# Attention followed by a squared-ReLU feed-forward network: value loads of 128 rows, early softmax work dealt anew, planner costs from occupied times

## The chip, the cores and the metric

The kernel runs on one core of a Trainium2 chip. The metric is the device time of one execution in microseconds (us), lower is better. Before the change three runs took 636.17, 637.12 and 638.25 us, median 637.12 us. The engines are named as in the profile: PE (TensorE matmul), PEld (its weight loads), DVE (VectorE), ACT (ScalarE), POOL (GpSimd) and SP (SyncE, which only issues DMAs here).

## The reference

```python
# attention: q, k, v are (4, 8, 768, 64) float32; block 32, window 16
k_sum = k.reshape(B, H, nb, block, D).max(axis=3)      # 24 block keys: the largest
v_sum = v.reshape(B, H, nb, block, D).mean(axis=3)     # 24 block values: the mean
scores_l = scale * q @ k^T, kept only where |i - j| < 16, else -1e9
scores_s = scale * q @ k_sum^T + log(32)
a = softmax(concat(scores_l, scores_s))                # 94 near keys and 24 block keys matter
x = a @ concat(v, v_sum)                               # -> 3072 tokens x 512
# feed-forward: w_in (512, 2048), w_out (2048, 512), drawn as 64-bit floats
h = x @ w_in ;  out = relu(h)**2 @ w_out               # (3072, 512) float32
```

## The kernel before

**Tiling.** A group g is 64 tokens of one batch with all 8 heads: 12 groups in each of 4 batches, 48 in all. A group needs 118 keys, the 24 block keys and 94 near ones. Eight groups (512 tokens) make a unit u of the feed-forward network, so there are 6 units; each runs over f = 0 to 15, blocks of 128 of the 2048 hidden columns. The start of the program has to push eight groups through attention before the first unit can run whole; its first half (groups 0 to 3) and the blocks f = 0 and 1 are taken in halves "a" and "b" so that something can start earlier.

**Attention of a group.** The names that the planner uses are given in brackets. SP loads the queries (QL, L442) and the values (LV, L449: 96 rows of 2 KB, into partitions 24 to 119 of the group's value tile). PE makes the scores (S, L486; for groups 0 to 7 it adds the mask by a second product). DVE takes the largest of each row (X, L557) and scales it (L561). ACT takes four exponentials with their sums (E, L573). DVE inverts the sums (R, L585 and L586). POOL multiplies (N, L592). PE transposes (T, L604) and ACT copies the result out (A, L611); from group 8 on DVE does the transposition instead (T, L621) with a round trip through memory. POOL copies the 24 block values into the value tile (LS, L455). PE multiplies by the values (V, L648). The result is split in two parts, a high part (XH, L700) and the rest (XL, L703). For groups 0 to 7, which are visited one at a time, both parts are made by DVE. The block values themselves are made once per batch by PE and gathered by four ACT copies (VS, L427); the block keys are made by four DVE reductions over the batch's keys (KL loads, L358; KM, L361).

**Feed-forward.** Weights come as 64-bit floats, 512 KB for each half of a block (WL, L747). They are turned into a high and a low part: ACT (WM, L750), DVE shift (WR, L753), DVE join (WJ, L759), ACT (WH, L764), DVE (WW, L767). PE then makes the hidden product (FI, L813: 12 matmuls), ACT applies ReLU and, in units 0 and 1, the square, ACT and DVE split the result (GH, L830; GL, L833), and PE makes the second product (FO, L843).

**What sets the order.** Each engine's instructions are written in the order that a small planner finds (`Plan.order`): a list scheduler over tasks with a cost, a key (a due time, the smaller the earlier), dependencies and buffers. It keeps a model of the DMA pipe (`DMA_RATE`, `DMA_LATENCY`). Due times come from `T0`, `STEP`, `A0`, `B0`, `HALF_AT`. The engines run their lists strictly in order, so a plan that is off by some time makes an engine wait behind one instruction. The DMA issues also follow each other in a ring: in the trace an issue starts when the eighth issue before it has landed, if that is later.

## Time and profile before

| | |
|---|---|
| time, median of 3 | 637.12 us |
| the profiled execution's own time | 635.87 us |
| its span | 634.2 us |
| PE busy | 613.0 us (97%) |
| DVE busy | 299.6 us (47%) |
| ACT busy | 268.7 us (42%) |
| POOL busy | 78.1 us (12%) |
| granted PE clock | 0.999 of full speed |

The span is from the first to the last instruction; the execution's own time is 1.67 us longer. Engines overlap, so the busy times do not add. A row of a timeline gives the start, the length, the engine, the line, the operation, output and inputs, and in brackets the idle time just before it with what ended it. The chip overlaps the end of one instruction with the start of the next on the same engine, so the time that one occupies is the distance of two starts where the engine is never idle, a little less than its length.

### The profile page before, as it was taken

What the parts mean: (1) busy time and instruction counts of PE and PEld (TensorE: products, weight loads), DVE (VectorE), ACT (ScalarE), POOL (GpSimd) and SP (SyncE); (2) the same over time, 40 slices, a digit from 0 to 9 for tenths busy, and PEclk for the clock granted to TensorE, in tenths of its full rate; (3) what the DMA queues carried; (4) which work ended last, traced back from release to release, by engine and by line L of the source; (5) the groups of instructions that cost most, each with busy time, mean ns of one, the idle gap of its engine ahead of it and who ended that gap; (6) DMA issues with size and microseconds to landing.
All of it is one profiled execution on the core that took longest, in us unless ns stands there. A gap on an engine that the chain in (4) does not pass through costs nothing.

```text
span 634.2 us, 11015 instructions
## 1 busy us (share of the span) xinstructions
PE 613.0 (97%) x4216; PEld 489.4 (77%) x4216; DVE 299.6 (47%) x517; ACT 268.7 (42%) x709; POOL 78.1 (12%) x140
## 2 busy tenths in 40 slices
PE   4779999999999999999999999999999999999997
PEld 3568788778777778777878778778788788888885
DVE  3798979633433433533543644534444432322221
ACT  1888778626544444332432523414343322222221
POOL 4731101101110110101210101201011010000000
PEclk9999999999999999999999999999999999999999
DMA  8998986244324832232415543133323020100001
GB/s 273 257 310 253 357 313 199 91 108 133 92 60 95 280 86 98 67 84 68 104 48 165 171 132 90 48 85 87 103 72 98 16 67 0 68 0 1 1 1 66
DMA packets 55448, 73.65 MB, mean 116 GB/s; under 512 B 6476, under 2 KB 33100, under 8 KB 55396
## 3 DMA queue, kind: packets, MB, share of 16 engines
q1 hardware_dynamic: 55396, 72.95, 39.0%
q8 instruction: 33, 0.54, 0.4%
q14 instruction: 19, 0.16, 0.1%
HBM read 55.56 MB, written 16.78 MB: 114 GB/s over the span
## 4 chain that ended last, share of the span: by engine, by line
PE 92%; DMA 7%; SPq 0%; DVE 0%; ACT 0%; issue 0%; DVEq 0%
PE o L843 42%; PE h L813 42%; PE x L648 3%; PE att L486 3%; DMA qvpa_lent<-qW 3%; DMA raw<-wW 2%; DMA q<-qW 1%; PE vps L415 1%; SPq L358 0%; PE h_0b L813 0%; PE h_1b L813 0%; DVE os L881 0%; ACT os L881 0%; DVE xl L703 0%; SPq L442 0%
## 5 line engine op out<-in xcount | busy, mean ns | idle before, releaser
L813 PE MATMUL h<-xh,w 128*128 128x512 f32 x752 | 236.9, 396 | 0.0
L843 PE MATMUL o<-w,gh 128*128 128x512 f32 x752 | 196.1, 395 | 1.4 <-DVE os L881 0.8
L843 PEld LDWEIGHTS o<-w,gh 128*128 128x128 f32 x752 | 139.7, 188 | 36.6 <-issue 2.7
L813 PEld LDWEIGHTS h<-xh,w 128*128 128x128 f32 x752 | 140.7, 188 | 33.8 <-issue 0.8
L813 PE MATMUL h<-xl,w 128*128 128x512 f32 x376 | 148.8, 396 | 0.0
L822 ACT ACTIVATE r<-h 128x512 f32<-128x512 f32 x94 | 56.2, 598 | 205.9 <-PE h L813 205.6
L833 DVE TENSOR_TENSOR gl<-r,gh 128x512 fp32r<-128x512 f32 x94 | 66.6, 709 | 101.6 <-ACT gh L830 65.5
L828 DVE TENSOR_TENSOR r<-r 128x512 f32<-128x512 f32 x64 | 45.2, 706 | 139.8 <-ACT r L822 139.7
L843 PE MATMUL o<-w,gl 128*128 128x512 f32 x376 | 106.4, 391 | 0.0
L813 PEld LDWEIGHTS h<-xl,w 128*128 128x128 f32 x376 | 70.6, 188 | 16.9
L843 PEld LDWEIGHTS o<-w,gl 128*128 128x128 f32 x376 | 70.6, 188 | 15.7
L830 ACT CAST gh<-r 128x512 fp32r<-128x512 f32 x94 | 58.3, 620 | 54.1 <-DVE r L828 27.8
L573 ACT ACTIVATE p<-p,nm 128x118 f32<-128x118 f32 x160 | 60.9, 383 | 30.8 <-DVE nm L557 30.7
L592 POOL TENSOR_TENSOR p<-p,nm 128x472 f32<-128x472 f32 x40 | 42.6, 1064 | 114.3 <-DVE nm L586 91.5
L496 POOL COPY kb<-kb 128x96 f32<-128x96 f32 x44 | 16.2, 368 | 306.1 <-PE att L486 282.7
L541 DVE SCALAR_TENSOR_TENSOR p<-att,mask 128x472 f32<-128x472 f32 x38 | 23.5, 644 | 27.8 <-PE att L486 27.8
L621 DVE STREAM_TRANSPOSE a<-p 128x512 f32<-128x512 f32 x40 | 28.3, 707 | 10.4 <-POOL p L592 9.0
L573 ACT ACTIVATION_READ_ACCUMULATOR p<-p,nm 128x1 f32 x160 | 30.0, 187 | 0.0
L557 DVE TENSOR_REDUCE nm<-p 128x4 f32<-128x472 f32 x40 | 25.0, 634 | 0.2
L486 PE MATMUL att<-kb,q 64*64 64x118 f32 x608 | 24.1, 274 | 0.0
L700 ACT CAST xh<-x 128x512 fp32r<-128x512 f32 x20 | 11.6, 582 | 28.6 <-PE x L648 28.6
L759 DVE SCALAR_TENSOR_TENSOR t<-t,raw 128x1024 uint32<-128x1024 uint32 (+1 forms) x19 | 21.8, 1148 | 3.5 <-ACT t L750 3.1
(104 smaller groups left out, 370.9 us busy)
## 6 DMA issues: line engine op xcount, KB each, us to landing
raw<-wW SPq DMA_DIRECT2D x32, 512.0 KB, 6.5
turn<-a SPq DMA_DIRECT2D x160, 64.0 KB, 1.8
a<-turn SPq DMA_DIRECT2D x40, 256.0 KB, 2.7
v<-vS SPq DMA_DIRECT2D x36, 192.0 KB, 3.2
kb<-kT SPq DMA_DIRECT2D x16, 384.0 KB, 4.8
out<-os SPq DMA_DIRECT2D x24, 256.0 KB, 2.2
q<-qW SPq DMA_DIRECT2D x40, 128.0 KB, 2.3
fv<-vS SPq DMA_DIRECT2D x18, 256.0 KB, 6.3
```

The costliest lines, as they stand in the source:

```text
L486: nc.tensor.matmul(score_tile(g)[c * TQ : (c + 1) * TQ, j, :], lhsT=q_bufs[g].tile[rows, p, :] if term else unscale[rows, :], rhs=kb[rows, ...
L541: nc.vector.scalar_tensor_tensor(out=pr.tile[:, js, :KEYS], in0=score_tile(g)[:, js], scalar=SCALE, in1=mask_of(g)[0].unsqueeze(1).broadca ...
L557: nc.vector.tensor_reduce(out=m, in_=score_tile(g)[:, js] if by_pe else pr.tile[:, js, :KEYS], op=ALU.max, axis=AX.X, negate=True)
L573: nc.scalar.activation(x, score_tile(g)[:, p] if by_pe else x, AF.Exp, bias=nm.tile[:, p : p + 1], scale=SCALE if by_pe else 1.0, accum_ou ...
L592: nc.gpsimd.tensor_tensor(out=x, in0=x, in1=nm.tile[:, 2 * NPAIR :].unsqueeze(2).broadcast_to([P, NPAIR, KEYS]), op=ALU.mult)
L621: nc.vector.transpose(out=a.tile.rearrange("p (j n r) -> p j n r", j=NSQ, n=NPAIR), in_=pr.tile.rearrange("p n (j c) -> p j n c", c=SQ),)
L813: nc.tensor.matmul(cut(h), lhsT=lhs.tile[:, k * P : (k + 1) * P], rhs=rhs[:, k, c0 : c0 + n], start=(i == 0), stop=(i == 3 * KT - 1),)
L822: t2 = add(f"RL{name}", "ACT", act, lambda: nc.scalar.activation(cut(r), cut(h), AF.Relu), due + 3, [t1], take=[r], use=[h])
L828: lambda: nc.vector.tensor_tensor(out=cut(r), in0=cut(r), in1=cut(r), op=ALU.mult), due + 4, [t2], use=[r],
L830: t4 = add(f"GH{name}", "ACT", act, lambda: nc.scalar.copy(out=cut(gh), in_=cut(r)), due + 5, [t3], take=[gh], use=[r])
L833: lambda: nc.vector.tensor_tensor(out=cut(gl), in0=cut(r), in1=cut(gh).bitcast(F32), op=ALU.subtract),
L843: nc.tensor.matmul(o_of(o, t), lhsT=terms[i][0].tile[:, (t - t0) * P : (t - t0 + 1) * P], rhs=terms[i][1].tile, start=(first and i == 0), ...
```

## The change

1. The values of groups 0 to 10 come from a second input, `vF`, which holds for each of these groups 128 rows: 24 empty ones, the 94 wanted, 10 empty ones. Each is loaded by one DMA of 128 rows instead of one of 96.
2. Groups 0 and 1 take their exponentials in another way (`ONE_EXP`): DVE subtracts the largest (D), ACT takes one exponential for all head pairs (for group 0 in two halves), DVE sums it (Z). The scaling at L561 falls away for them.
3. The high part XH goes to ACT for groups 2 to 7 (`HIGH_DVE`), DVE keeps groups 0 and 1. The four gathering copies of batch 0 (VS) go from ACT to DVE.
4. The planner's costs become smaller for most tasks, its DMA rate larger, and its due times earlier.

```diff
@@ constants, the planner, due times
+HIGH_DVE = 2
+ONE_EXP = 2
-    HOP, DMA_LATENCY, DMA_RATE = 0.12, 1.9, 300e3
+    HOP, DMA_LATENCY, DMA_RATE = 0.12, 1.9, 370e3
-    T0, SLOW, STEP, LEAD = 33.0, 6.6, 6.0, 1.5
+    T0, SLOW, STEP, LEAD = 29.0, 6.6, 6.0, 1.5
-            t_K[b].append(add(f"KM{b}_{p}", "DVE", 0.945, lambda p=p: top(p), key + 0.1 * p, [t]))
+            t_K[b].append(add(f"KM{b}_{p}", "DVE", 0.85, lambda p=p: top(p), key + 0.1 * p, [t]))
...
@@ block values of batch 0
-                nc.scalar.copy(out=vs.tile[:, c * P : (c + 1) * P], in_=out_ps.tile[c * SQ : c * SQ + NB, :P])
+                copy(out=vs.tile[:, c * P : (c + 1) * P], in_=out_ps.tile[c * SQ : c * SQ + NB, :P])
+        copy = nc.scalar.copy if b else nc.vector.tensor_copy
+        t_VS[b] = [add(f"VS{b}", "ACT" if b else "DVE", 1.1, gather, key + 7, [last], take=[vs], use=[out_ps])]
@@ values
+            if g < vF.shape[0]:
+                nc.sync.dma_start(out=vv.tile, in_=vF[g])
+                return
@@ softmax
-                if by_pe:
+                if by_pe and not one:
                     nc.vector.tensor_scalar_mul(m, m, SCALE)
+            def less(js=js, nj=nj):
+                nc.vector.tensor_tensor(
+                    out=pr.tile[:, js, :KEYS], in0=score_tile(g)[:, js],
+                    in1=nm.tile[:, :NPAIR][:, js].unsqueeze(2).broadcast_to([P, nj, KEYS]), op=ALU.add,
+                )
+            def exp(js=js):
+                e = pr.tile[:, js, :KEYS]
+                nc.scalar.activation(e, e, AF.Exp, scale=SCALE)
+            def total(js=js):
+                nc.vector.tensor_reduce(
+                    out=nm.tile[:, NPAIR : 2 * NPAIR][:, js], in_=pr.tile[:, js, :KEYS], op=ALU.add, axis=AX.X
+                )
+            if one:
+                t_d = add(f"D{name}", "DVE", 0.07 + 0.49 / parts, less, due - 12.9, [t_x[-1], t_c], use=[s, nm, pr])
+                t_e1 = add(f"E{name}", "ACT", 0.18 + 0.28 / parts, exp, due - 12, [t_d], use=[pr])
+                t_e.append(add(f"Z{name}", "DVE", 0.07 + 0.48 / parts, total, due - 11.5, [t_e1], use=[pr, nm]))
@@ the high part
-            (nc.vector.tensor_copy if n == 1 else nc.scalar.copy)(out=by_group(xh), in_=x_all())
+            (nc.vector.tensor_copy if g < HIGH_DVE else nc.scalar.copy)(out=by_group(xh), in_=x_all())
@@ the new input
+    vF = np.zeros((EARLY + NV, P, H * D), v.dtype)
+    for g in range(EARLY + NV):
+        k0 = first_key(g, S)
+        vF[g, S // BLOCK : S // BLOCK + LOC] = vS[0, k0 : k0 + LOC]
```

**What moves on the engines.** On PE the set of blocks ahead of FI 0_0b (the second half of unit 0, block 0) is the same before and after, only dealt in another order. SP's list has the same order up to its 33rd row. Three places on DVE show the rest.

The first is DVE between the largest of group 2 and the inverse of group 2; nm1, nm2, nm3 belong to groups 1, 2, 3, raw0_0 is the first weight block. Before:

```order
L557 TENSOR_REDUCE nm2_296<-s2_260 128x4
L561 TENSOR_SCALAR nm2_296<-nm2_296 128x4
L585 TENSOR_SCALAR nm1_255<-nm1_255 128x4
L586 RECIPROCAL nm1_255<-nm1_255 128x4
L557 TENSOR_REDUCE nm3_341<-s3_315 128x4
L561 TENSOR_SCALAR nm3_341<-nm3_341 128x4
L753 TENSOR_SCALAR raw0_0_172<-raw0_0_172 128x512
L585 TENSOR_SCALAR nm2_296<-nm2_296 128x4
```

And now:

```order
L578 TENSOR_TENSOR qvpa1_lent_114<-s1_216,nm1_255 128x4x118
L566 TENSOR_REDUCE nm2_295<-s2_259 128x4
L570 TENSOR_SCALAR nm2_295<-nm2_295 128x4
L430 COPY vs0_305<-vps0_202 24x128 x4
L588 TENSOR_REDUCE nm1_255<-qvpa1_lent_114 128x4
L781 TENSOR_SCALAR raw0_0_175<-raw0_0_175 128x512
L614 TENSOR_SCALAR nm1_255<-nm1_255 128x4
L615 RECIPROCAL nm1_255<-nm1_255 128x4
L566 TENSOR_REDUCE nm3_352<-s3_311 128x4
L570 TENSOR_SCALAR nm3_352<-nm3_352 128x4
L614 TENSOR_SCALAR nm2_295<-nm2_295 128x4
```

The difference and the sum of group 1 and the four copies came in; the shift of the first weights stands two tasks earlier.

The second is DVE up to the rest (XL) of group 7, the last part of the first unit's input; a8 is the transposed softmax of group 8, raw3 the weights of block 3. Before:

```order
L833 TENSOR_TENSOR gl0_0a_698<-r0_0a_652,gh0_0a_683 128x256
L753 TENSOR_SCALAR raw0_2_408<-raw0_2_408 128x512
L541 SCALAR_TENSOR_TENSOR p1_79<-s9_623,mask1_72 128x4x118
L585 TENSOR_SCALAR nm8_646<-nm8_646 128x4
L586 RECIPROCAL nm8_646<-nm8_646 128x4
L759 SCALAR_TENSOR_TENSOR t0_2_655<-t0_2_655,raw0_2_408 128x512
L700 CAST xh_69<-att_66 128x4x64
L557 TENSOR_REDUCE nm9_723<-p1_79 128x4
L621 STREAM_TRANSPOSE a8_729<-p0_78 128x512
L703 TENSOR_TENSOR xl_70<-att_66,xh_69 128x4x64
```

And now:

```order
L795 TENSOR_TENSOR w1_1_657<-t1_1_626,w1_1_657 128x512
L550 SCALAR_TENSOR_TENSOR p1_79<-s9_601,mask1_72 128x4x118
L781 TENSOR_SCALAR raw3_476<-raw3_476 128x1024
L732 TENSOR_TENSOR xl_70<-att_66,xh_69 128x4x64
L861 TENSOR_TENSOR gl0_0a_702<-r0_0a_670,gh0_0a_698 128x256
L566 TENSOR_REDUCE nm9_705<-p1_79 128x4
L614 TENSOR_SCALAR nm8_637<-nm8_637 128x4
L615 RECIPROCAL nm8_637<-nm8_637 128x4
L732 TENSOR_TENSOR xl_70<-att_66,xh_69 128x4x64
```

The casts to xh of groups 2 to 7 are gone from DVE, the transposition of group 8 went behind XL of group 7, and the shift of block 3 came ahead of it.

The third is DVE in front of the low part of block 6's weights (w6), which PE needs for FI 0_6; the kb rows are the block keys of batch 1, nm10 and nm11 belong to groups 10 and 11. Before:

```order
L541 SCALAR_TENSOR_TENSOR p1_79<-att_66,mask2_73 128x4x118
L759 SCALAR_TENSOR_TENSOR t6_980<-t6_980,raw6_810 128x1024
L585 TENSOR_SCALAR nm10_986<-nm10_986 128x4
L586 RECIPROCAL nm10_986<-nm10_986 128x4
L557 TENSOR_REDUCE nm11_1026<-p1_79 128x4
L753 TENSOR_SCALAR raw7_876<-raw7_876 128x1024
L621 STREAM_TRANSPOSE a10_1032<-p0_78 128x512
L759 SCALAR_TENSOR_TENSOR t7_1022<-t7_1022,raw7_876 128x1024
L767 TENSOR_TENSOR w6_1036<-t6_980,w6_1036 128x2x512
L361 TENSOR_REDUCE kb_68<-kb_68 128x24 x3
```

And now:

```order
L566 TENSOR_REDUCE nm11_990<-p1_79 128x4
L787 SCALAR_TENSOR_TENSOR t6_978<-t6_978,raw6_814 128x1024
L614 TENSOR_SCALAR nm10_982<-nm10_982 128x4
L615 RECIPROCAL nm10_982<-nm10_982 128x4
L781 TENSOR_SCALAR raw7_877<-raw7_877 128x1024
L364 TENSOR_REDUCE kb_68<-kb_68 128x24
L650 STREAM_TRANSPOSE a10_1033<-p0_78 128x512
L364 TENSOR_REDUCE kb_68<-kb_68 128x24 x3
L614 TENSOR_SCALAR nm11_990<-nm11_990 128x4
L615 RECIPROCAL nm11_990<-nm11_990 128x4
L795 TENSOR_TENSOR w6_1026<-t6_978,w6_1026 128x2x512
```

The four reductions of the keys and the inverse of group 11 now stand ahead of w6, the join of block 7 behind it.

## Rows read from the trace of the kernel before

**Rows 1.** Busy time by stretch: from:to and length, engines with instructions, clock, DMA, GB/s.

```profile
30.00:40.00 10.00, 8.43 (x146) 7.18 (x146) 9.82 (x23) 7.80 (x26) 4.68 (x8) 1.00 1.05 291
40.00:50.00 10.00, 7.11 (x57) 5.80 (x56) 9.93 (x23) 9.69 (x31) 3.47 (x3) 1.00 0.97 327
50.00:60.00 10.00, 10.00 (x45) 8.06 (x44) 9.66 (x14) 8.12 (x14) 0.00 (x0) 1.00 0.76 214
```

**Rows 2.** PE's waits from 46 us on: us in total, times, longest.

```profile
PE h_0b L813 <- DVE xl L703: 1.1, 1, 1.1
PE o L843 <- DVE os L881: 0.8, 1, 0.8
PE o L843 <- ACT os L881: 0.6, 1, 0.6
```

**Rows 3.** Timeline of PE: the third matmul of FI 0_0b, FI 0_3, FI 0_6.

```profile
46.25 0.39 PE L813 MATMUL h_0b<-xl,w 128*128 128x256 f32 x1 [1.05 <-DVE xl L703]
...
54.54 0.63 PE L813 MATMUL h<-xh,w 128*128 128x512 f32 x2
...
74.36 0.62 PE L813 MATMUL h<-xh,w 128*128 128x512 f32 x2
```

**Rows 4.** Timeline of DVE, 16 to 48 us.

```profile
16.24 0.65 DVE L557 TENSOR_REDUCE nm<-s 128x4 f32<-128x472 f32 x1 [0.45 <-PE s L486]
...
18.74 0.65 DVE L557 TENSOR_REDUCE nm<-s 128x4 f32<-128x472 f32 x1 [1.24 <-PE s L486]
...
20.77 0.43 DVE L753 TENSOR_SCALAR raw<-raw 128x512 uint32<-128x512 uint32 x1 [1.02 <-DMA raw<-wW]
21.11 0.16 DVE L585 TENSOR_SCALAR nm<-nm 128x4 f32<-128x4 f32 x1
...
23.09 0.41 DVE L700 CAST xh<-att 128x256 fp32r<-128x256 f32 x1
23.43 0.52 DVE L585 TENSOR_SCALAR nm<-nm 128x4 f32<-128x4 f32 x1
...
27.90 0.80 DVE L753 TENSOR_SCALAR raw<-raw 128x512 uint32<-128x512 uint32 x1 [0.30 <-DMA raw<-wW]
...
45.17 0.71 DVE L621 STREAM_TRANSPOSE a<-p 128x512 f32<-128x512 f32 x1
...
47.04 0.69 DVE L753 TENSOR_SCALAR raw<-raw 128x1024 uint32<-128x1024 uint32 x1
```

**Rows 5.** Timeline of SP's queue: first weight block, key loads of batch 1.

```profile
12.09 0.35 SPq L747 DMA_DIRECT2D raw<-wW  x1
...
65.34 2.16 SPq L358 DMA_DIRECT2D kb<-kT  x4
```

**Rows 6.** Busy time by stretch, columns as in rows 1.

```profile
5.00:10.00 5.00, 2.00 (x20) 1.26 (x20) 2.98 (x6) 0.00 (x0) 2.48 (x11) 1.00 0.96 337
...
15.00:20.00 5.00, 4.63 (x112) 3.37 (x104) 2.89 (x10) 4.33 (x22) 3.54 (x7) 1.00 1.06 233
```

**Rows 7.** Timeline of ACT, a cast of 128x256.

```profile
40.83 0.40 ACT L830 CAST gh_0a<-r_0a 128x256 fp32r<-128x256 f32 x1
```

**Rows 8.** Timeline of DVE, 52 to 77 us.

```profile
52.30 1.22 DVE L767 TENSOR_TENSOR w<-t,w 128x1024 fp32r<-128x1024 f32 x1
...
64.29 0.64 DVE L541 SCALAR_TENSOR_TENSOR p<-att,mask 128x472 f32<-128x472 f32 x1
...
70.44 1.18 DVE L759 SCALAR_TENSOR_TENSOR t<-t,raw 128x1024 uint32<-128x1024 uint32 x1
71.54 1.21 DVE L767 TENSOR_TENSOR w<-t,w 128x1024 fp32r<-128x1024 f32 x1
72.67 2.65 DVE L361 TENSOR_REDUCE kb<-kb 128x24 f32<-128x768 f32 x3
...
76.37 0.91 DVE L833 TENSOR_TENSOR gl<-r,gh 128x512 fp32r<-128x512 f32 x1
```

**Rows 9.** The tile kb from 60 to 80 us: issue of its loads to landing.

```profile
DMA to landing us min/median/max: 5.7/5.7/5.7
```

More of the change, by code (lines that the diff above doesn't have):

```diff
@@ L426, in gather @@
             for c in range(NSQ):
-                nc.scalar.copy(out=vs.tile[:, c * P : (c + 1) * P], in_=out_ps.tile[c * SQ : c * SQ + NB, :P])
-        t_VS[b] = [add(f"VS{b}", "ACT", 1.1, gather, key + 7, [last], take=[vs], use=[out_ps])]
+                copy(out=vs.tile[:, c * P : (c + 1) * P], in_=out_ps.tile[c * SQ : c * SQ + NB, :P])
+        copy = nc.scalar.copy if b else nc.vector.tensor_copy
+        t_VS[b] = [add(f"VS{b}", "ACT" if b else "DVE", 1.1, gather, key + 7, [last], take=[vs], use=[out_ps])]
     t_QL, s_bufs = {}, {}
@@ L465, in loads @@
             else:
-                lv.append(add(f"LS{g}", "POOL", 0.45, copy_s, due - 19, ts + lv, use=[vv, vs_bufs[b]]))
+                lv.append(add(f"LS{g}", "POOL", 0.62, copy_s, due - 8, ts + lv, use=[vv, vs_bufs[b]]))
     def mask_of(g):
@@ L527, in softmax @@
         nm = buf("nm", 3, (P, 3 * NPAIR), F32, f"nm{g}")
-        t_m, t_x, t_c = [], [], None
+        t_m, t_x, t_e, t_c = [], [], [], None
+        one = g < ONE_EXP
         if g < EARLY + 2:
@@ L576, in exps @@
             )
-        t_e = [
-            add(f"E{g}_{p}", "ACT", 0.39, lambda p=p: exps(p), due - 12 + 0.1 * i, [t_x[p % parts], t_c], use=[pr, nm] + [s] * by_pe)
+        t_e = t_e or [
+            add(f"E{g}_{p}", "ACT", 0.335 if by_pe else 0.38, lambda p=p: exps(p), due - 12 + 0.1 * i, [t_x[p % parts], t_c], use=[pr, nm] + [s] * by_pe)
             for i, p in enumerate(sorted(range(NPAIR), key=lambda p: p % parts))
@@ L586, in inverse @@
             nc.vector.reciprocal(out=rec, in_=rec)
-        t_r = add(f"R{g}", "DVE", 0.36, inverse, due - 10.5, t_e, use=[nm])
+        t_r = add(f"R{g}", "DVE", 0.3, inverse, due - 10.5, t_e, use=[nm])
         def normal():
@@ L594, in normal @@
             )
-        t_n = add(f"N{g}", "POOL", 1.03, normal, due - 10, [t_r], use=[pr, nm])
+        t_n = add(f"N{g}", "POOL", 1.0, normal, due - 10, [t_r], use=[pr, nm])
         if wide:
@@ L614, in turned @@
                 )
-            t_A[g] = add(f"A{g}", "ACT", 0.6, turned, due - 8.5, [t_T[g]], take=[] if early else [a], use=[at_ps] + [a] * early)
+            t_A[g] = add(f"A{g}", "ACT", 0.47, turned, due - 8.5, [t_T[g]], take=[] if early else [a], use=[at_ps] + [a] * early)
         else:
@@ L626, in softmax @@
             assert not early
-            t_T[g] = add(f"T{g}", "DVE", 0.72, turn, due - 9, [t_n], take=[a], use=[pr])
+            t_T[g] = add(f"T{g}", "DVE", 0.63, turn, due - 9, [t_n], take=[a], use=[pr])
             d = buf("turn", 4, (NSQ, SQ, NSQ, NPAIR * SQ), F32, f"turn{g}", dr)
@@ L705, in low @@
             )
-        g = both[-1]
-        t_h = add(f"XH{g}", "DVE" if n == 1 else "ACT", 0.13 + 0.24 * n, high, due + 0.5, [t_v], use=[x_ps])
-        t_l = add(f"XL{g}", "DVE", 0.15 + 0.27 * n, low, due + 1, [t_h], use=[x_ps])
+        t_h = add(f"XH{g}", "DVE" if g < HIGH_DVE else "ACT", (0.334 if n == 1 else 0.48), high, due + 0.5, [t_v], use=[x_ps])
+        t_l = add(f"XL{g}", "DVE", 0.06 + 0.27 * n, low, due + 1, [t_h], use=[x_ps])
         for g in both:
@@ L776, in convert @@
             ))
-        t2 = add(f"WM{name}", "ACT", 0.16 + 0.54 * k, rebias, due - 8, t1, take=[t], use=[raw])
-        t3 = add(f"WR{name}", "DVE", 0.1 + 0.37 * k, rest, due - 8, t1, use=[raw])
-        t4 = add(f"WJ{name}", "DVE", 0.13 + 0.56 * k, join, due - 7, [t2, t3], use=[raw, t])
-        t6 = add(f"WH{name}", "ACT", 0.1 + 0.52 * k, high, due - 6, [t4], take=[w], use=[t])
-        t7 = add(f"WW{name}", "DVE", 0.13 + 0.56 * k, low, due - 4.5, [t6], use=[w, t])
+        t2 = add(f"WM{name}", "ACT", 0.02 + 0.5 * k, rebias, due - 8, t1, take=[t], use=[raw])
+        t3 = add(f"WR{name}", "DVE", 0.09 + 0.27 * k, rest, due - 8, t1, use=[raw])
+        t4 = add(f"WJ{name}", "DVE", 0.03 + 0.54 * k, join, due - 7, [t2, t3], use=[raw, t])
+        t6 = add(f"WH{name}", "ACT", 0.08 + 0.43 * k, high, due - 6, [t4], take=[w], use=[t])
+        t7 = add(f"WW{name}", "DVE", 0.07 + 0.53 * k, low, due - 4.5, [t6], use=[w, t])
         for i, n in enumerate(ns):
@@ L880, in put @@
         t1 = add(
-            f"PC{u}_{t}", "ACT" if k else "DVE", 0.62 if k else 0.7, lambda: copy(out=part(), in_=o_tile()), due + 0.6, [t6],
+            f"PC{u}_{t}", "ACT" if k else "DVE", 0.48 if k else 0.6, lambda: copy(out=part(), in_=o_tile()), due + 0.6, [t6],
             take=[] if k else [x], use=[o] + [x] * k, behind=t_PC[-1] if k else None,
```

17 lines of the change are left out of this document (10 added, 7 removed).

## The prediction

> **What bounds the kernel now.** I read the busy time by stretch first [rows 1]: from 50 us on PE is busy 10.00 of 10 us, while DVE, at 9.82 and 9.93 of 10, was the full engine from 30 to 50. Then PE's waits [rows 2]: from 46 us on there are three in the whole program, 1.1, 0.8 and 0.6 us. So the time is a start, in which eight groups go through attention, plus a fixed amount of PE work that runs without a hole. Where the start ends is seen in PE's timeline [rows 3]: the third matmul of FI 0_0b, at 46.25, waited for the rest (XL) of group 7. The order shows the same set of PE blocks ahead of FI 0_0b before and after. So the change is worth what XL of group 7 moves, less any hole that PE gets behind it. DVE writes XL and was never idle long ahead of it, so I add up DVE's work.
>
> The sum goes against the profiled execution, 635.87 us. That run was 1.25 us below the median of the three, 637.12; I take the difference from the median. A difference below 0.3% (1.9 us) is what measuring this kernel cannot tell from none.
>
> **Part 1, DVE up to the inverse of group 2.** In this stretch DVE stood idle 0.45, 1.24 and 1.02 us, 2.71 in all [rows 4]. New in it are D of group 1 (the nearest row is a 128x472 elementwise of 0.64 [rows 8]), Z of group 1 (a 128x472 reduction of 0.65 [rows 4]) and the four copies of block values. Those copies have no row on DVE. From below, half of the 0.34 that a 128x256 cast occupies (23.09 to 23.43 [rows 4]) gives 0.7 for four; from above the whole gives 1.4. They are half as wide, so I take 0.8. Together 2.1 us go into 2.71 us of idle time: the inverse of group 2, at 21.11 before, comes 0.6 us earlier. Bounds: 1.0 earlier if all of it hides, 0 if the copies cost 1.4. D and Z of group 0 and the dropped scalings lie in front of that, where DVE waits for PE's scores; they gain nothing, since the largest of group 2 still waits for its scores at 16.24. What pays in ACT's shorter list there is only room.
>
> **Part 2, DVE from there to XL of group 7.** Six casts XH leave DVE: 6 x 0.34 = 2.0 us less. The transposition of group 8 (0.71) goes behind XL of group 7, the shift of block 3 (0.69) comes ahead of it [rows 4]: even. On ACT the six casts cost 6 x 0.40 = 2.4 us [rows 7]. Between 30 and 40 us ACT is idle for 2.2 of 10 us [rows 1], and the four copies and some exponentials left it earlier, so I cost them at nothing. That cover ends at 40 us, where ACT was busy 9.69 of 10: if the last two casts fall there, XL waits up to 0.8 us. The new wait is XL for ACT's cast; behind XL on DVE stand the weight joins that PE needs next.
>
> **Part 3, the loads.** DVE can only use idle time if the weights are there. The first block was issued at 12.09 [rows 5] and DVE, which waited for it, began at 20.77 [rows 4]: 8.7 us. In this time the DMA engines were full, share 1.06, but moved 233 GB/s, whereas from 5 to 10 us, with loads of 128 rows, they moved 337 at a share of 0.96 [rows 6]. If the 128-row loads bring the second rate, 8.7 us become 8.7 x 233/337 = 6.0, plus 0.4 for two loads that are 64 KB longer: 18.5. DVE gets there at about 18.6, so no wait. The second block is issued when the first has landed and took until 27.90, 7.1 us: 7.1 x 0.69 + 0.8 for four longer loads = 5.7, so 24.2. DVE wants it between 23.4 and 24.1 (20.5, plus the tasks up to it at their row lengths, the join lengthened by POOL or not). That is a wait of 0.1 to 0.8 against 0.30 before: 0.1 us worse.
>
> This is the one place where rule and rule disagree. The rows say that the same full engines move 337 or 233 GB/s, and that the slow stretch is the one with loads of 96 rows. The Trainium skill, page "DMA: Bandwidth & Descriptors", section "Why a DMA increments its semaphore by 16 and not by 1", says that a tile of 96 partitions is spread over 16 engines just as one of 128 is. By that alone the wider loads use no more engines and only add 64 KB each, which is the third rival below. The skill's page "SBUF — State Buffer", section "Door 1: The DMA port swizzle", says that the partition number decides the memory port and that the rate follows the ports reached; rows put at partition 24 and up then do not fall on one port per engine, which would fit the slow stretch. No row names ports.
>
> **Sum of the start:** -0.6 - 2.0 + 0.1 = -2.5 us. XL of group 7 ends at about 43.7 instead of 46.2.
>
> **Part 4, what is late next.** FI 0_3 (54.54 [rows 3]) needs the low part of block 3, which ended at 52.30 + 1.22 = 53.5 [rows 8]: 1.0 us to spare. Between XL of group 7 and this task the new order has a transposition, one more shift of a whole block and one more GL, less the shift of block 3: about 1.0 us more. The spare time is gone, the hole is 0.1 (bounds 0 and 0.6, if a POOL task holds DVE).
>
> FI 0_6 (74.36 [rows 3]) needs the low part of block 6. Before, DVE began the softmax of group 10 at 64.29, right after it had what PE gave it, and ended this low part at 72.67, 8.38 us later. The new order takes the join of block 7 out of this stretch (70.44 to 71.54, 1.10) and puts in the four key reductions and an inverse (72.67 to 76.37, 3.70) [rows 8]. So 64.29 + 8.38 - 1.10 + 3.70 = 75.27, on the old clock, and PE has a hole of 0.9 us in front of FI 0_6. This holds wherever the start ends, since PE sets the begin of the stretch. From below 0.3, if the shift of block 7 (lengthened beside POOL before) is not. From above: the key loads were issued at 65.34 [rows 5] and took 5.7 us [rows 9], so 71.0; the first reduction would want them at 64.29 + 8.38 - 1.10 - 1.13 - 0.71 = 69.7. Half a weight block that was queued ahead of them is queued behind them now, so I take no wait, and 1.2 more as the bound. FI 0_7 and the values of group 11 follow with the same distance as before or more, and need nothing on top.
>
> Total: -2.5 + 0.1 + 0.9 = -1.5 us. In the profile about 634.4, as a median 635.6.
>
> **The rivals.**
> The gain stays whole: the key loads and the shift of block 7 are quicker, POOL holds DVE less, and the hole in front of FI 0_6 is at most 0.2 us while the start moves 3 us: 637.1 - 3 = 634.1. For it: DVE's idle time ahead of 21 us was 0.6 us larger than what goes in. Against: block 6 had 1.7 us to spare before and 2.6 us of work were put ahead of it.
>
> The gain is paid back: the new order has less spare time throughout, since its costs equal the times the engines were busy, and each lengthened DVE task becomes a hole. Then the hole at FI 0_6 is 2.1 us (with the wait for the keys), at FI 0_3 0.6: 637.1 - 2.5 + 2.7, about 637.3. For it: only three holes before, at larger costs. Against: PE that waits makes everything behind it easier.
>
> The loads do not speed up (the slower side). At 233 GB/s the first block lands at 20.77 + 0.6 = 21.3, the second at 21.3 + 7.1 + 1.1 = 29.5. DVE, in order, waits there; what follows up to XL of group 7 was 25.1 us from 21.11 on, less 2.0, less the 3.3 done before that wait and the 0.3 of old wait: 19.5. XL of group 7 ends at 49.0, 2.8 late, and with the hole of 0.9 the time is 640.8. It decides as soon as the second block lands after about 26.7 (24.2 + 2.5), a rate below some 290 GB/s from 10 us on. Against: 337 from 5 to 10 us, and 327 from 40 to 50 [rows 1], where few 96-row loads are left. For it: query loads of small rows stand in the slow stretch too, and stay.
>
> **How the numbers follow.** Forecast (634.6 to 636.6) 0.38; gain whole 0.30; paid back 0.16; loads not faster 0.16. Faster by over 0.3% means below 635.2: the second case and a third of the first, 0.43. Slower means above 639.0: the last case and a little of the third, 0.18. The rest, 0.39, is within. The range from 632.8 (DVE gains its 1.0, no hole, ACT's cover holds) to 638.8 leaves out most of the last case. The likeliest case lies within what is hard to tell from none.
>
> **What would show it.** Right: the rate from 15 to 25 us above 300 GB/s; no wait of DVE for the first weight block, a small one for the second; the casts of groups 2 to 7 on ACT; XL of group 7 ends at 43 to 44; a wait of PE for the low part of block 6, about 1 us. Wrong: a rate near 240, or XL of group 7 at 46 or later (Parts 1 to 3); PE without a hole from 44 to 100 us (Part 4); ACT late with XH of groups 6 and 7 (Part 2).

## The result and the profile after

| | before | after |
|---|---|---|
| time, median of 11 runs | 637.12 us | 639.65 us |
| lowest to highest | 634.58 to 638.6 | 637.67 to 641.83 |
| ratio after to before | | 1.0043, 95% interval 1.0025 to 1.0062 |
| profiled execution, its span | 635.87, 634.2 | 637.67, 636.0 |

The change makes the kernel slower by some 2.5 us. The forecast was 635.6, with 632.8 to 638.8 as its range; the time lies outside, on the side that had a chance of 0.18. The profiled execution of after was the quickest of its eleven, so what follows shows the loss at its smallest: 1.8 us.

**The loads did speed up.** Busy time by stretch, after; columns as in [rows 1].

```profile
15.00:20.00 5.00, 4.22 (x113) 3.11 (x106) 4.74 (x15) 3.14 (x12) 3.59 (x6) 1.00 1.03 370
20.00:25.00 5.00, 3.54 (x72) 2.70 (x72) 4.93 (x10) 4.61 (x20) 4.18 (x6) 1.00 1.05 371
25.00:30.00 5.00, 3.32 (x72) 2.47 (x72) 4.86 (x14) 3.42 (x13) 3.97 (x7) 1.00 1.03 403
30.00:35.00 5.00, 2.65 (x55) 2.16 (x56) 4.88 (x9) 4.12 (x20) 3.93 (x6) 1.00 0.87 303
35.00:40.00 5.00, 4.16 (x48) 3.68 (x47) 4.42 (x10) 4.59 (x11) 1.76 (x5) 0.73 0.93 323
40.00:45.00 5.00, 5.00 (x57) 4.54 (x56) 4.32 (x11) 4.16 (x18) 0.73 (x1) 0.93 0.42 160
```

The last column says 370 GB/s from 15 to 20 us where [rows 6] had 233, at the same full engines. Two columns ahead of it stands a thing that before did not have: the granted clock of PE falls to 0.73 and 0.93, behind a stretch in which PE was busy 2.65 of 5 us.

**The start gained less than forecast.** Timeline of DVE, first three rows of before (the second part of group 0's largest, the inverse of group 2, XL of group 7), then after; it answers to [rows 4].

```profile
11.86 0.40 DVE L557 TENSOR_REDUCE nm<-s 128x2 f32<-128x236 f32 x1 [1.15 <-PE s L486]
...
21.31 0.18 DVE L586 RECIPROCAL nm<-nm 128x4 f32<-128x4 f32 x1
...
45.81 0.38 DVE L703 TENSOR_TENSOR xl<-att,xh 128x256 fp32r<-128x256 f32 x1
```
```profile
11.19 0.40 DVE L566 TENSOR_REDUCE nm<-s 128x2 f32<-128x236 f32 x1 [1.15 <-PE s L494]
...
17.76 0.47 DVE L781 TENSOR_SCALAR raw<-raw 128x512 uint32<-128x512 uint32 x1
...
19.98 0.18 DVE L615 RECIPROCAL nm<-nm 128x4 f32<-128x4 f32 x1
...
24.19 1.09 DVE L795 TENSOR_TENSOR w<-t,w 128x512 fp32r<-128x512 f32 x1
...
30.01 1.44 DVE L795 TENSOR_TENSOR w<-t,w 128x512 fp32r<-128x512 f32 x1
...
37.59 0.42 DVE L732 TENSOR_TENSOR xl<-att,xh 128x256 fp32r<-128x256 f32 x1 [0.47 <-PE att L677]
...
40.02 0.68 DVE L795 TENSOR_TENSOR w<-t,w 128x512 fp32r<-128x512 f32 x1
...
42.52 0.42 DVE L732 TENSOR_TENSOR xl<-att,xh 128x256 fp32r<-128x256 f32 x1 [0.65 <-ACT xh L729]
...
44.04 0.40 DVE L732 TENSOR_TENSOR xl<-att,xh 128x256 fp32r<-128x256 f32 x1
```

The first weight block is shifted at 17.76 without a wait (20.77 before). The last row is XL of group 7: it ends at 44.4, not 43.7; before it was 46.2. PE's timeline, after, shows the next loss: FI 0_0b starts 0.5 us after that, since PE's own list is late (it runs without a break from 37.41 to there).

```profile
34.72 0.66 PE L633 MATMUL t<-ident,qvpa_lent 128*128 128x128 f32 x4 [1.70 <-POOL qvpa_lent L621]
...
38.18 0.78 PE L841 MATMUL h_0a<-xh,w 128*128 128x256 f32 x2
...
44.93 0.41 PE L841 MATMUL h_0b<-xh,w 128*128 128x256 f32 x2
...
46.37 0.40 PE L841 MATMUL h_1b<-xh,w 128*128 128x256 f32 x2
```

and before:

```profile
47.53 0.40 PE L813 MATMUL h_1b<-xh,w 128*128 128x256 f32 x2
```

FI 0_1b starts 1.16 us earlier than before, not 2.5. At 38.18 a pair of half matmuls takes 0.78 where it takes 0.40 at 46.37: that is the low clock.

**Behind the start PE has new holes.** Timeline of PE, after; before, none of these places had a wait.

```profile
53.39 0.92 PE L841 MATMUL h<-xh,w 128*128 128x512 f32 x2
54.15 0.39 PE L841 MATMUL h<-xl,w 128*128 128x512 f32 x1
...
73.51 0.39 PE L841 MATMUL h<-xh,w 128*128 128x512 f32 x1
74.96 0.50 PE L841 MATMUL h<-xh,w 128*128 128x512 f32 x1 [1.06 <-DVE w L795]
...
80.39 0.39 PE L841 MATMUL h<-xh,w 128*128 128x512 f32 x1
81.24 0.50 PE L841 MATMUL h<-xh,w 128*128 128x512 f32 x1 [0.46 <-DVE w L795]
...
88.77 0.63 PE L494 MATMUL att<-kb,q 64*64 64x118 f32 x16 [0.27 <-POOL kb L504]
```

The distance from the first to the second matmul is 0.23 when nothing waits, so FI 0_6 loses 74.96 - 73.51 - 0.23 = 1.2 us, FI 0_7 0.6 and the scores of group 13 0.3. FI 0_3, at 53.39, loses 0.3: its first two matmuls take 0.76, such a pair without a wait 0.47. What holds the low part of block 6 is on DVE, after; it answers to [rows 8].

```profile
67.68 0.68 DVE L781 TENSOR_SCALAR raw<-raw 128x1024 uint32<-128x1024 uint32 x1
68.75 0.95 DVE L364 TENSOR_REDUCE kb<-kb 128x24 f32<-128x768 f32 x1 [0.39 <-DMA kb<-kT]
69.61 0.70 DVE L650 STREAM_TRANSPOSE a<-p 128x512 f32<-128x512 f32 x1
70.24 1.77 DVE L364 TENSOR_REDUCE kb<-kb 128x24 f32<-128x768 f32 x2
72.55 0.95 DVE L364 TENSOR_REDUCE kb<-kb 128x24 f32<-128x768 f32 x1 [0.54 <-DMA kb<-kT]
73.42 0.16 DVE L614 TENSOR_SCALAR nm<-nm 128x4 f32<-128x4 f32 x1
73.62 0.18 DVE L615 RECIPROCAL nm<-nm 128x4 f32<-128x4 f32 x1
73.71 1.20 DVE L795 TENSOR_TENSOR w<-t,w 128x1024 fp32r<-128x1024 f32 x1
```

The key reductions stand ahead of w6 and wait 0.39 and 0.54 us for keys that took 6.8 us to land (5.7 in [rows 9]).

**The balance.** I compare the moments at which ACT takes the same hidden block from PE. It is -1.14 us at FI 0_1b, -0.86 at FI 0_4 (FI 0_3 had a hole of 0.3), +1.63 at FI 1_12, and +1.78 near the end. Between FI 0_4 and FI 1_12 all PE work is the same; by the distances between its starts, the hidden products take 2.1 us more there, and the wait in front of the scores of group 13 is the other 0.3. So a start that had gained 1.1 us was followed by a loss of 0.3 and 2.5.

### The profile page after: what moved, and what is told of

It reads as the page before. It is cut to its first block, busy times and chain, and to the rows that moved or that the text cites. A ratio compares the mean times of both kernels' runs of the same rounds, so it can differ in the third digit from the quotient of the medians.

```text
span 636.0 us, 10999 instructions
## 1 busy us (share of the span) xinstructions
PE 614.1 (97%) x4216; PEld 490.4 (77%) x4216; DVE 302.0 (47%) x518; ACT 267.9 (42%) x698; POOL 80.1 (13%) x140
## 4 chain that ended last, share of the span: by engine, by line
PE 92%; DVE 3%; DMA 2%; issue 1%; SPq 1%; ACT 1%; POOL 0%; DVEq 0%; POOLq 0%
PE o L871 41%; PE h L841 41%; PE att L494 3%; PE x L677 3%; DMA kb<-kT 1%; DMA raw<-wW 1%; PE vps L418 1%; PE s L494 1%; DVE nm L566 0%; PE h_0a L841 0%; DMA turn<-a 0%; PE att L677 0%; POOL kb L504 0%; PE h_1a L841 0%; ACT qvpa_lent L602 0%
## 5 line engine op out<-in xcount | busy, mean ns | idle before, releaser
L795 DVE TENSOR_TENSOR w<-t,w 128x1024 fp32r<-128x1024 f32 (+1 forms) x19 | 22.0, 1157 | 2.6 <-ACT w L792 2.6
L677 PE MATMUL x<-a,v 118*64 118x64 f32 x640 | 23.0, 225 | 0.0
```

Of the source, the lines that this page charges most:

```text
L677: nc.tensor.matmul(x_of(i)[h % 2 * D : (h % 2 + 1) * D, h // 2, :], lhsT=v_bufs[g].tile[:KEYS, h * D : (h + 1) * D], rhs=av[:KEYS, 2 * c : ...
```

## The experiments

Times are medians; each ratio is to the kernel before, timed beside it on the same chip, so ratios rather than times are to be compared. The kernels that change an order keep the planner's own result: a function takes the emitted list, puts a task ahead of another one of its engine, and merges the five lists again; the pairs are shown (the moved task, then the one that it now precedes; WW6 is task WW of block 6). Nothing else in the order moves.

### The loads

`loads_alone`, on the kernel before, and `old_loads`, on the changed one:

```diff
+            if g < vF.shape[0]:
+                nc.sync.dma_start(out=vv.tile, in_=vF[g])
+                return
```
```diff
-            if g < vF.shape[0]:
+            if False:
```

> The kernel before with the 128-row value loads of the first eleven groups alone; the order of every instruction on every engine is that of the kernel before. Theory A (the loads do bring the first weight blocks earlier, and what the whole change loses is lost elsewhere: in TensorE's clock and in holes behind the start): the transfers between 15 and 25 us run at over 350 GB/s instead of 233 and 252, VectorE's wait for the first block goes, XL7 ends 1.5 to 2.5 us earlier than 46.2 and the time is 634.6 to 635.6. Rival B (earlier blocks are worth nothing, since TensorE has other work to wait for): 637.1, within 0.5. Rival C (more rows cost bandwidth that something else misses): 638 and above.

> The changed kernel with the 96-row loads of before, in the changed kernel's order. Theory A: the rate between 15 and 25 us falls back to about 240 GB/s, VectorE stands for the first block at 17.8 us until about 21.5, and the time is 2 to 3.5 us over the changed kernel's: 641.6 to 643.2. Rival B (the loads are worth nothing): 639.7, within 0.5. Rival C (the wide loads themselves cost): below 639.

`loads_alone` took 635.63 us, ratio 0.9964 (0.9947 to 0.9982): theory A. Busy time by stretch:

```profile
15.00:20.00 5.00, 4.32 (x103) 3.31 (x99) 3.37 (x12) 4.94 (x25) 4.49 (x8) 1.00 1.05 383
20.00:25.00 5.00, 4.25 (x103) 3.32 (x98) 4.86 (x13) 4.43 (x18) 4.22 (x9) 1.00 1.05 390
```

With the order of before and only the loads changed, the rate goes from 233 and 252 to 383 and 390 GB/s. The number of rows and the first partition (0 instead of 24) changed together; which of them does it, no run shows. The Trainium skill, page "DMA: Bandwidth & Descriptors", section "Why a DMA increments its semaphore by 16 and not by 1", gives a tile of 96 partitions the same 16 engines as one of 128; by that alone the rate would have stayed. The rows agree as far as the engines go, whose share was full both times (1.06 and 1.05), but the rate did not stay.

`old_loads` took 640.82 us, ratio 1.0051 (1.0030 to 1.0073), against 1.0043 for the change: between the two theories' bands, nearer to B. The rate fell (283 and 285 GB/s) and DVE waited 1.56 us for a weight block; in the profile XL of group 7 came 1.2 us later than in after, counted from the second part of group 0's largest. Yet the ratio moved by 0.08%, less than the intervals can tell. So the same loads are worth 0.36% in one order and nothing that can be told in the other. Does something behind the start swallow what the start gains?

### The hole at block 6

`w6_first`, on the changed kernel (moved task, the task it now precedes):

```diff
+    ("WW6", "KM1_0"), ("T10", "KM1_0"), ("WJ7", "KM1_0"), ("R11", "KM1_2"),
+    ("GL0_5", "KM1_2"), ("WW7", "KM1_2"), ("T11", "KM1_2"), ("WH7", "WM8"),
```

> The changed kernel with VectorE's order changed between 68 and 78 us alone: the low part of weight block 6 ahead of the key reductions of the second batch, blocks 7's join and low part ahead of the last two of them, and one cast of ACT (block 7's) ahead of block 8's first pass. Theory A (TensorE's two holes at 74 and 81 us come from VectorE's order there and are paid in full): both waits for w are gone, 1.2 and 0.6 us, and the time is 1.8 us under the changed kernel's, 637.9, between 637.4 and 638.3. Rival B (the gain is given back further on, at the next block or at the scores of group 12): 639.2 to 639.7, with a new wait of TensorE between 85 and 110 us.

638.11 us, ratio 1.0013 (0.9996 to 1.0030): theory A, 0.3% below the change (the two intervals just overlap). Timeline of DVE:

```profile
68.99 1.65 DVE L843 TENSOR_TENSOR w<-t,w 128x1024 fp32r<-128x1024 f32 x1 [0.27 <-ACT w L840]
...
72.29 1.80 DVE L412 TENSOR_REDUCE kb<-kb 128x24 f32<-128x768 f32 x2
```

The low part of block 6 comes at 68.99 instead of 73.71, the keys behind it need not be waited for, and PE's waits for w at 74 and 81 us are gone.

### PE's clock

`pe_padded`, on the changed kernel, and `w6_padded`, the same on `w6_first`:

```diff
+            def pad(n):
+                for _ in range(n):
+                    nc.tensor.matmul(at_ps.tile[:, :P], lhsT=ident, rhs=ident, start=True, stop=True)
             def turn():
+                pad({4: 2, 6: 10}.get(g, 0))
...
+            if t.name == "V5":
+                pads[0][0].make()
+                pads[0][1](5)
```

> The changed kernel with 17 extra 128x128 matmuls on TensorE, put where it waits (2 ahead of the transposes of group 4, 10 ahead of those of group 6, 5 ahead of group 5's values); they write a tile that the transposes then overwrite. They are extra work, so nothing gets earlier by them but by the clock. Theory A (the granted clock falls to half behind 30 us because TensorE had stood for much of 25 to 38 us, and the runs differ in how long it stays there): granted clock 0.998 or more in every run instead of 0.991 to 0.996, the first hidden pass of the halved block 1.5 us instead of 2.74, the time 637 to 638.7 and the runs closer together. Rival B (the clock's fall has another cause, or the start is VectorE's in any case and the clock is hidden by it): 639.7, within 0.5; and if the extra matmuls stand in the way, up to 641.

> w6_first with the 17 extra matmuls of pe_padded. Theory A (the fallen clock costs 1 us or more at the end of the start): granted clock 0.998 or more in all runs, FI0_0a in 1.5 us, and 0.7 to 1.5 us under w6_first: a ratio of 0.9990 to 1.0002. Rival B (VectorE sets the start's end all the same, the slow stretch of TensorE is mostly hidden by it): the ratio of w6_first, 1.0013, within 0.0006, though the clock is up.

`pe_padded`: 638.74 us, ratio 1.0028 (1.0005 to 1.0050), between the two bands. `w6_padded`: 638.25 us, ratio 1.0027 (1.0010 to 1.0044), against 1.0013 without the padding: outside theory A's band, and above rival B's. The granted clock of the whole program was 0.998 or more in 10 and in 9 of 12 executions, not in all as theory A had it, and the runs of `pe_padded` did not come closer together (636.25 to 643.96). Busy time by stretch, PE and DVE, `w6_padded`:

```profile
30.00:35.00 5.00, 4.31 (x85) 3.65 (x78) 4.90 (x12) 4.12 (x18) 3.47 (x4) 1.00 0.97 339
35.00:40.00 5.00, 5.00 (x65) 4.49 (x65) 3.54 (x9) 3.87 (x11) 2.32 (x6) 1.00 0.87 283
40.00:45.00 5.00, 4.95 (x58) 4.33 (x58) 4.96 (x12) 4.71 (x18) 0.05 (x1) 1.00 0.56 208
```
```profile
39.24 0.49 PE L897 MATMUL h_0a<-xh,w 128*128 128x256 f32 x2
...
45.04 0.40 PE L897 MATMUL h_0b<-xh,w 128*128 128x256 f32 x2
```
```profile
39.02 0.42 DVE L788 TENSOR_TENSOR xl<-att,xh 128x256 fp32r<-128x256 f32 x1 [1.37 <-PE att L733]
...
43.21 0.42 DVE L788 TENSOR_TENSOR xl<-att,xh 128x256 fp32r<-128x256 f32 x1
```

The clock stays at 1.00 and FI 0_0a takes 1.5 us instead of 2.7. But the padding costs something itself: the five matmuls ahead of group 5's values hold these up, and DVE, at XL of group 4, waits 1.37 us for a value product, where after waited 0.47 (the row at 37.59). At XL of group 6 the wait of 0.65 (42.52) is gone. Counted from the inverse of group 2, XL of group 7 comes 0.16 us later than in after and in `w6_first`, and FI 0_0b 0.41 us sooner (24.54 instead of 24.95). So the low level did cost the start something, 0.4 us or more in these profiles, since the extra matmuls only add work; and the two ratios do not give its price, which stays open.

The executions of one kernel, compared with each other, show that time goes with the clock. Of 103 executions of the kernel before, timed beside these experiments, 21 had a granted clock of 0.998 or more; their median is 634.9 us. Another 45 had 0.993 or less, and their median is 637.4. In the changed kernel the two at 0.996 took 637.7 and 638.3 us, the two below 0.993 took 640.8 and 641.8. Which moves the other no run tells: in the profiles of the changed kernel and its variants the low level follows waits of PE in the start, and a start that is late for another reason has more of them. The clock does not make the change slower, since at the same 0.993 the kernel before took 637.3 (21 executions) and the changed one 640.5 (3). But it bears on comparisons of a few tenths of a per cent. Of the 11 executions of `loads_alone`, four had 0.998 or more, with a median of 633.9 us, where the kernel before took 635.3 on that chip (4); seven had 0.996, with 635.9, where it took 636.6 (7). At like clocks the loads are worth 0.7 to 1.5 us, a little less than the 1.65 of the medians.

### What the casts are worth

`casts_back` on the changed kernel, `loads_casts` on `loads_alone`:

```diff
-            (nc.vector.tensor_copy if g < HIGH_DVE else nc.scalar.copy)(out=by_group(xh), in_=x_all())
+            (nc.vector.tensor_copy if g < UG else nc.scalar.copy)(out=by_group(xh), in_=x_all())
```
```diff
-            (nc.vector.tensor_copy if n == 1 else nc.scalar.copy)(out=by_group(xh), in_=x_all())
+            (nc.vector.tensor_copy if g < 2 else nc.scalar.copy)(out=by_group(xh), in_=x_all())
```

> The changed kernel with the casts of groups 2 to 7 on VectorE again, each at its place in the order; everything else as changed. Theory A (of the casts' 2.0 us that VectorE got rid of, little reached the end: it waits 1.1 us for ACT's casts, and what it then does ahead of XL7 is a block's low part more): XL7 ends at most 1 us later, and the time is 639.2 to 640.4. Rival B (the casts were worth their 2.0 us, and the start lost as much elsewhere): 641 to 642. Rival C (the hand-over to ACT costs more than the casts): below 639.2.

> The kernel before with the 128-row loads and with the casts of groups 2 to 7 on ACT, each at the place that it had among all instructions; two parts of the change, in the order of before. Theory A (VectorE is busy to the end of the start, but ACT is as well, and the last casts wait behind its exponentials and first passes): XL7 within 0.7 us of that of the loads alone, the time 635 to 636.2. Rival B (the casts are worth 1.5 to 2 us to the start): 633.6 to 634.4. Rival C (hand-overs to ACT cost more than the casts): over 636.3.

`casts_back`: 640.97 us, ratio 1.0074 (1.0052 to 1.0096), 0.3% above the change (again with a small overlap); the kernel before took 636.11 beside it, which makes it rival B, not A. XL of group 7 starts at 46.41 instead of 44.04; PE's low level lasted twice as long in this profile as in that of after, so a part of the difference may be the clock's. `loads_casts`: 634.41 us, ratio 0.9979 (0.9965 to 0.9994), no better than the loads alone (0.9964); by the ratio this is theory A. PE, `loads_casts`:

```profile
42.82 0.50 PE L817 MATMUL h_0b<-xh,w 128*128 128x256 f32 x2 [0.80 <-ACT xh L704]
44.14 0.39 PE L817 MATMUL h_0b<-xl,w 128*128 128x256 f32 x1 [0.82 <-DVE xl L707]
```

The last cast waits on ACT now, behind the exponentials of group 8. The casts are worth some 2 us where the order was made for them, and nothing that can be told where it was not.

### The copies, on ACT and by DMA

`copies_on_act` and `values_by_dma` on the changed kernel, `w6_copies` on `w6_first`:

```diff
-        copy = nc.scalar.copy if b else nc.vector.tensor_copy
+        copy = nc.scalar.copy
```
```diff
-                lv.append(add(f"LS{g}", "POOL", 0.62, copy_s, due - 8, ts + lv, use=[vv, vs_bufs[b]]))
+                lv.append(add(f"LS{g}", "POOL", 0.62, copy_s if g < 3 else load_s, due - 8, ts + lv, use=[vv, vs_bufs[b]]))
```

> The changed kernel with the four copies of the block values (VS0) on ACT as before, at their place in the order. Theory A (on VectorE they cost their 1.1 us in full, since VectorE does not wait behind them any more): XL7 ends 0.7 to 1.1 us earlier and the time is 638.5 to 639.1. Rival B (as the prediction had it: they fill time in which VectorE would wait, now for ACT's exponentials): 639.7, within 0.4.

> w6_first with the four copies of the block values on ACT again. Theory A (the copies on VectorE cost up to 1.1 us, and only the hole at block 6 hid it in copies_on_act): 0.5 to 1.1 us under w6_first, a ratio to the kernel before of 0.9995 to 1.0005. Rival B (they fill time in which VectorE would wait): the ratio of w6_first, 1.0013, within 0.0005.

> The changed kernel, but the block values of groups 3 to 7 are brought by a DMA each instead of by a copy on GpSimd (24x512, 0.6 to 1.07 us); everything else, the order too, as changed. Theory A (VectorE's shifts and low parts of 0.68 took 1.09 to 1.44 beside these copies, which is what ate the gain of the casts): between the inverse of group 2 and XL7 VectorE gets through 1 to 1.5 us sooner, and the time is 638.2 to 639.0, with the holes at weight block 6 still there. Rival B (VectorE is lengthened by GpSimd's products and key copies, not by these copies, or waits elsewhere): 639.7, within 0.5. Rival C (the DMAs come later than the copies and TensorE waits for values): over 640.3.

`copies_on_act`: 639.40 us, 1.0045 (1.0028 to 1.0063). `w6_copies`: 638.37 us, 1.0026 (1.0011 to 1.0042). `values_by_dma`: 639.61 us, 1.0044 (1.0026 to 1.0061). None shows a gain: the first and the last lie in rival B's band, `w6_copies` lies above its own, and its interval holds it. DVE and PE of `copies_on_act`, then PE of `values_by_dma`, show why the hole matters:

```profile
69.66 0.95 DVE L364 TENSOR_REDUCE kb<-kb 128x24 f32<-128x768 f32 x1 [1.52 <-DMA kb<-kT]
```
```profile
75.65 0.50 PE L841 MATMUL h<-xh,w 128*128 128x512 f32 x1 [1.98 <-DVE w L795]
```
```profile
31.30 1.98 PE L677 MATMUL att<-qvpa_lent 118*64 118x64 f32 x32 [2.53 <-ACT qvpa_lent L602]
...
76.59 0.50 PE L841 MATMUL h<-xh,w 128*128 128x512 f32 x1 [3.24 <-DVE w L795]
```

In the profiles of the changed kernel and its variants without `w6_first`, the wait at FI 0_6 was 0.7 to 3.2 us, longest where PE came there early or the keys late. In `values_by_dma` DVE's shifts and low parts were 0.8 us shorter in the start, so part of that theory holds. But PE waited 2.53 us in front of a value product: the row names ACT's exponentials, which that product does not read; its transposed softmax was there at 29.84, and of the block values, whose DMA was issued at 25.52, the last piece landed at 31.16. And where PE then came early to FI 0_6 it stood.

### Orders of the start

`start_and_w6`, on `w6_first` (the first two lines), and `loads_order_3`, on `loads_alone` (the others). `loads_order` and `loads_order_2` share its first three pairs and the late block 1_2, and place ACT's casts otherwise; `loads_order_2_dma` adds the edit of `values_by_dma`. The halves of weight block 2 are called 0_2 and 1_2.

```diff
+    ("XH3", "E7_0"), ("XL3", "WJ1_0"), ("FI0_0a", "T6"), ("RL0_0a", "A6"),
+    ("WM3", "E9_0"), ("WJ3", "WR1_2"), ("WH3", "RL0_0b"), ("WW3", "WR4"),
...
+    ("A7", "WH1_1"), ("XH7", "WR0_2"), ("XL7", "WR0_2"), ("WR1_2", "GL0_2"), ("WJ1_2", "GL0_2"), ("WW1_2", "WR6"),
+    ("T9", "WW3"), ("WR4", "GL0_0b"), ("WW6", "T10"), ("RL0_0b", "E9_0"), ("SQ0_0b", "WM4"),
+    ("WM1_2", "WH4"), ("WH1_2", "GH0_3"), ("WM5", "RL0_3"), ("RL0_4", "WH5"), ("SQ0_4", "WH5"), ("WH6", "E11_0"),
```

> The changed kernel with the order of w6_first behind 60 us and another order in the start: ACT's cast of group 3 ahead of group 7's exponentials, VectorE's low part XL3 ahead of a weight join, the first hidden pass FI0_0a on TensorE ahead of group 6's transposes (where TensorE stood for 1.7 us), and block 3's chain ahead of groups 8 and 9. Theory A (in the start TensorE's order and its clock cost beside VectorE): FI0_0a runs at the full clock in some 1.5 us and ends by 35.5, the first hidden pass of half b begins 0.5 to 1.4 us earlier, FI0_3 has no hole, and the time is 636.3 to 637.4, that is 0.7 to 1.8 us under w6_first's 638.1. Rival B (VectorE alone sets the start's end, TensorE's order in it costs nothing): 638.1, within 0.4.

> The kernel before with the 128-row loads, and three moves in its order: group 7's turned copy on ACT ahead of a weight cast, group 7's cast and low part on VectorE ahead of the shift of block 0_2 instead of behind two group steps and a transpose, and block 1_2 (wanted at 61 us) behind block 4 on both engines. Nothing else. Theory A (with the loads early, what ends the start is VectorE's order, since it is busy throughout and TensorE waits 0.66 and 1.05 us for group 7): XL7 ends 2 to 3 us earlier than with the loads alone, TensorE has no wait between 40 and 60 us, and the time is 633.2 to 634.6. Rival B (what the start gains is given back where the later blocks are converted and loaded, 60 to 90 us): 635 to 636, with new waits of TensorE for w there.

> The kernel before with the 128-row loads and some moves in its order, such that ACT does not stand for late casts as it did in loads_order: group 7's turned copy ahead of a weight cast; its cast and low part ahead of the shift of block 0_2; VectorE's work for block 1_2 behind block 4; casts of blocks 3, 4 and 6 on ACT earlier; group 9's transposition behind two shifts; block 6's low part ahead of group 10's transposition. Theory A (VectorE's order ends the start, and the blocks behind it have 1 us to spare that these moves keep): TensorE waits nowhere for over 0.3 us between 40 and 90 us, the half pass FI0_0b begins 1.5 to 2.3 us earlier than with the loads alone, and the time is 633 to 634.3. Rival B (the gain is given back at blocks 3 to 6, or to ACT): 635 to 636.

> The same with the block values of groups 3 to 7 brought by DMAs instead of copies on GpSimd. Theory A (these copies lengthen VectorE's work in the start): 0.5 to 1.3 us below loads_order_2. Rival B: the same as loads_order_2, within 0.4. Rival C (the DMAs are late or delay the weight loads behind them in their queue): over 0.5 us above it.

> The kernel before with the 128-row loads and moves in its order as in loads_order_2, but ACT's first passes go ahead of the weight casts that wait for VectorE, and the low part of block 1_2 comes after the joins that ACT wants. Theory A (VectorE's order ends the start, and loads_order_2 lost its gain to ACT, which stood 0.75, 2.4 and 2.1 us in front of such casts): TensorE's waits of 0.64 and 1.58 us at 50 and 63 us are gone, and the time is 0.5 to 1.5 us below that of the loads alone: a ratio of 0.9940 to 0.9956. Rival B (the next wait takes its place, at blocks 3 to 6): the ratio of the loads alone, 0.9964, or above.

| | us | ratio, 95% interval |
|---|---|---|
| start_and_w6 | 636.70 | 1.0006 (0.9992 to 1.0021) |
| loads_order | 635.37 | 1.0000 (0.9984 to 1.0015) |
| loads_order_2 | 635.14 | 0.9985 (0.9974 to 0.9996) |
| loads_order_2_dma | 638.64 | 1.0042 (1.0027 to 1.0056) |
| loads_order_3 | 634.16 | 0.9956 (0.9940 to 0.9972) |

`start_and_w6` is not to be told from `w6_first`, though its first hidden passes went into the gap of PE, its clock was 0.997 or more in all twelve executions, and FI 0_0b came 1.7 us sooner behind the inverse of group 2 (23.27 instead of 24.95); a new wait of 0.64 us at 57.81 took part of it. The first two orders on the loads missed: from the inverse of group 2 to XL of group 7 they took 22.0 us instead of 24.7, and the next wait took it back. ACT, `loads_order_2`, stood in front of casts whose joins DVE had not done, with the first passes that PE waited for behind them:

```profile
53.76 1.05 ACT L823 CAST w<-t 128x1024 fp32r<-128x1024 f32 x1 [2.43 <-DVE t L818]
...
61.53 1.05 ACT L823 CAST w<-t 128x1024 fp32r<-128x1024 f32 x1 [2.05 <-DVE t L818]
```

DMAs for the block values made it worse: PE waited 3.75 us for a DMA in front of a value product at 29 us. `loads_order_3` clears ACT's list, leaves PE one wait of 0.29 us between 42 and 125 us, and is the quickest version run here: below the kernel before and below the change. That it beats the loads alone (0.9964) the intervals do not show. All its ten executions had a granted clock of 0.998 or more; the six of the kernel before that had it on that chip took 635.3, so at like clocks its lead is 1.2 us, not the 2.8 of the medians.

## Why the prediction was wrong

The forecast was -1.5 us, and the profiles show +1.6 at FI 1_12. Of these 3.1 us, 1.4 lie in the start, which gave 1.1 for 2.5 at FI 0_1b, and 1.8 behind it, where 2.8 were lost for 1.0.

Each start begins with the first keys. How late they came shows in the row for the second part of group 0's largest, which begins between 10.5 and 11.9 us in the profiles: 11.86 in that of before, 11.19 in that of after. The changed kernel and `w6_first`, alike up to 60 us, had 11.19 and 11.62, so this is not the change's doing, and I measure from that row. It also means that 0.67 us of the 1.1 at FI 0_1b was luck. By that estimate the profile's loss of 1.8 us would be 2.5 without it, as that of the medians is.

| us from that row | before | loads_alone | after | casts_back |
|---|---|---|---|---|
| to the inverse of group 2 | 9.45 | 8.18 | 8.79 | 8.43 |
| from there to XL of group 7 | 24.50 | 24.65 | 24.06 | 27.09 |

- **Part 1** (-0.6) was right: 8.79 - 9.45 = -0.66. The loads alone would have given -1.27; the rest of the change takes 0.6 of that back. Of its terms the four copies were too low, 1.1 us (16.11 to 17.21) for 0.8.
- **Part 3** was right: over 300 GB/s, no wait of DVE for the first block, and none for the second, where 0.1 to 0.8 was forecast.
- **Part 2 failed in its size**: -2.0 became -0.44. I take the distances between starts on DVE in this stretch. The casts took 2.15 us less, as forecast. But DVE waited 0.82 more for ACT's casts and PE's values (the text had 0.8 as the bound, and counted nothing), the low parts took 1.05 more and the 512-wide shifts 1.02 more, since others of them now fell beside GpSimd (the rows at 24.19 and 30.01 above, 1.09 and 1.44 against 0.68). The shift of block 3 added 0.69; the transposition (-0.64), the joins (-0.53), the inverses with the scalings (-0.49) and small things took 1.87 off. The step that failed is the one from "Six casts XH leave DVE" to a stretch that is 2.0 us shorter: it gave all tasks that stayed the lengths that they had before, and ACT's cover no price. But they were dealt anew, and their lengths depend on what GpSimd does beside them.
- **Left out of the sum**: PE's own list and its clock. FI 0_0a moved behind a wait of 1.70 us for group 6's product and ran at half the clock. In after FI 0_0b starts 0.5 us behind XL of group 7 for that; in `w6_padded`, with the clock up, it starts as XL of group 7 ends.
- **Part 4 failed**, and it is the larger part of the loss. FI 0_6 lost 1.2 us, forecast 0.9; the wait for the keys, which the text held possible as a bound, came. FI 0_7, which "need nothing on top", lost 0.6; the scores of group 13, which the text does not name, 0.3; FI 0_3 0.3 for 0.1. Together that is 2.4 against 1.0. "This holds wherever the start ends, since PE sets the begin of the stretch" was the wrong sentence: the keys set it. In `copies_on_act` and `values_by_dma` FI 0_0b came 1.1 and 0.5 us sooner than in after, counted from the first keys' row, and the wait at FI 0_6 was longer for it, 1.98 and 3.24 us instead of 1.06. The wait is not fixed either: in `old_loads` and `casts_back` FI 0_0b came 1.2 and 1.8 us later, and it was 2.07 and 1.77, since the keys came later still. `w6_first` gives 0.3% back.
- **The rivals**: the one with the right cause was "The gain is paid back" (637.3), with its price too low. "Loads not faster" came nearer in time (640.8), for a reason that the rates exclude.

Not settled: with the holes of block 6 gone, `w6_first` is still not faster than before, though `loads_alone` is. In its profile PE's scores and values up to FI 1_12 take 0.95 us more than before; no run took that away alone. `loads_casts` (0.9979) differs from the changed kernel (1.0043) by the other softmax of groups 0 and 1, the copies and the new order. `copies_on_act` shows no price for the copies, so the softmax and the order together cost 0.6%; no run separates these two.
